# A second record of TensorE's activity, and zero matmuls by it, in a four-layer attention kernel

## The chip, the core and the metric

The kernel runs on one core of one Trainium2 chip, as one launch. A core has five engines that run at the same time, each through its own list of instructions: TensorE (PE in the profile; its weight loads are the row PEld), ScalarE (ACT), VectorE (DVE), GpSimd (POOL) and SyncE (SP, which here only issues DMAs). They wait for one another by semaphores. The metric is the device time of one execution in microseconds (us). TensorE's clock is not constant: the profile has a record of the share of the full clock that was granted, called the granted clock here.

## What is computed

Four layers act on x of 2048 tokens by 512 features (32 heads of 16 features), each adding to x. Layers 0 and 2 are kind A: causal softmax attention within segments of 512 tokens, plus a linear-attention memory of the earlier segments. Layers 1 and 3 are kind B: full softmax attention over all 2048 tokens.

```
x = x + A(layernorm(x)); x = x + B(layernorm(x))
x = x + A(layernorm(x)); x = x + B(layernorm(x))

B: q, k, v = split(x @ wqkv)
   p = softmax(q k^T * 0.25);  o = p v;  return o @ wo
A: per segment s of 512 tokens, with the running memory M, z:
   a_dot = softmax(q k^T * 0.25 + causal mask) v
   a_mem = (phi(q) M) / (phi(q) z + 1e-6)
   o = g * a_mem + (1 - g) * a_dot;  then M += phi(k)^T v, z += sum(phi(k))
   return o @ wo
```

Nearly all of the work is the exponentials: 32 heads by 2048 by 2048 scores in each B layer.

## The kernel before

Every instruction is recorded first, in Python, and only then written to the engines. The class `Sched` keeps for each engine a list of operations and a clock `t` of when the engine would be through by the kernel's own estimates (`estimate`, line 95). `add` (line 123) finds what an operation must wait for from the buffers and the PSUM banks it touches. `Builder.attention` (line 1759) decides the order by comparing these estimated clocks, so that whatever moves an estimated clock also moves the order of the rest. The constants of those decisions are replaced every 40 us or so of estimated time (`PIECES`, line 271).

The work is cut into groups (`Group`, line 227): one layer, one segment of 512 queries, one chunk of eight heads and one half of those heads. A group is a list of score blocks, each 128 keys by 512 queries of one head. The main loop runs in steps. Each step makes one unit (`unit`, line 1454):

- three score blocks on TensorE, each a matmul that uses 32 rows of the array (`ps<-qm,KA` or `ps<-qm,KB` in the profile), into three PSUM banks; two sets of three banks alternate,
- one or two ScalarE instructions that take the exponential of the banks into `pT` (line 1514),
- for kind A the causal mask on GpSimd (line 1529).

VectorE makes a part of the exponentials itself, in the tiles `dxw`, from score blocks that go to separate banks (lines 1121 and 1184). Two units later the value matmuls take `pT` and `dxw` into the accumulating bank `ACC` (`pv`, line 1556): in the last layers with 17 columns of the array and 512 streamed rows (`128*17`), else with the whole array and 34 or 51 rows. The list `pvq` holds what is still due, and `g.left` counts the value matmuls that a group still lacks. Projections, layer norms, the memory and the output projection are background tasks, run between units (`background`, `bg_one`) as far as the estimated clocks leave room. Q, K and V are held in SBUF; DMA transposes move `xn`, `ob`, `KA` and `amem` between their two layouts.

At the end of each step stands `keep_busy` (line 429). It adds matmuls whose weights are the all-zero tile `zero`, so that they add zero to the accumulating bank, or write to a free one when no group is accumulating. It does so while the recorded streaming time of TensorE in the last 3413 ns, kept in `streams`, is under the share `FILL`, and at most `FILLS` times a step. In `streams` a matmul on 32 rows counts 0.285 of its streaming time, one on 17 columns 0.38. These zeros go through `add` like any other matmul: they move TensorE's estimated clock and so what the builder does next. All matmuls are recorded in one helper, `mm`, at line 445. A zero matmul shows in the profile as `ps<-wB,zero`.

Of the kernel before, what the change touches and what calls it, by code (L numbers as in the profile page):

```python
# [22 lines left out]
UNIT, DXB, ACC = (0, 4), 3, 7  # L23
# [6 lines left out]
class Op:  # L30
    __slots__ = ("eng", "idx", "fn", "deps", "emit", "evno", "is_dma", "batch", "name", "end")

    def __init__(self, eng, idx, fn, name=""):
        self.eng = eng
        self.idx = idx
        self.fn = fn
        self.deps = []
        self.emit = False
        self.evno = None
        self.is_dma = False  # L40
        self.batch = None
        self.name = name
        self.end = 0.0
# [35 lines left out]
class Sched:  # L79


    def __init__(self):
        self.ops = {e: [] for e in ENGS}
        self.t = {e: 0.0 for e in ENGS}
        self.tiles = []

        self.streams = []

    def streamed(self, until, ns):

# [4 lines left out]
    def estimate(self, op, ns, gap, tile):  # L95
        e = op.eng
        ready = max([d.end + LAG[d.eng] if d.eng != e else d.end + 35 for d in op.deps], default=0.0)
        if tile is not None:
            rows, r0, cols, c0, n = tile
            st = max(ready, self.pe_issue())  # L100
            if cols < 128:
                st = max(st, self.pe_issue() + 30)
            for i, (a, ar, b, bc, m, at) in enumerate(self.tiles):
                if ar < r0 + rows and r0 < ar + a and bc < c0 + cols and c0 < bc + b:
                    after = 104 if (a, b) != (rows, cols) else 5 if cols == 128 else 4
                    if after == 5 and rows == 128 and 0 < i == len(self.tiles) - 1 and self.tiles[i - 1][0] == 32:
                        after += 13
                    st = max(st, at + m / 2.4 + after)
            self.tiles = self.tiles[-11:] + [(rows, r0, cols, c0, n, st)]
            self.t["pe"] = max(self.t["pe"], st + n / 2.4)  # L110
            self.streams.append((st, n / 2.4 * (0.285 if rows < 128 else 0.38 if cols < 128 else 1)))
            op.end = st + n / 2.4 + 170
        elif e == "sp":
            st = max(ready, self.t[e])
            self.t[e] = st + max(gap, 600)
            op.end = st + ns
        else:
            op.end = self.t[e] = max(self.t[e] + gap, ready + ns)
# [139 lines left out]
class Builder:  # L258
# [170 lines left out]
    def keep_busy(self):  # L429


        g, n = self.cur, 0
        own = g is not None and g.npv
        if not own and (self.bank_late() > 0 or any(t["next"][0][:1] == ["cont"] for t in self.tasks)):
            return
        bank, al = (self.banks[ACC], g.acc) if own else (self.banks[DXB], self.new_alloc())
        soon = [w.end + LAG[w.eng] for e in self.pvq[:9] if e[0] <= self.unit_no + 1 for w in (self.b_pT[e[4] * 3 + e[5]].last_write,)]
        at = max(self.sc.t["act"] - 1330, min(soon, default=0.0) - self.HOR)
        while n < self.FILLS and self.sc.streamed(max(self.sc.t["pe"], at), 3413) < self.FILL:
            self.mm(self.ps[:, bank.col0:bank.col0 + 512], self.zero[:, :], self.wB[:, 0, 0:512], not own, not own,  # L440
                    [self.b_zero, self.b_wB[0]], bank, al, "fill")
            n += 1

    def mm(self, out, lhsT, rhs, start, stop, reads, bank, alloc, name="", tile=(128, 0, 128, 0), n=512):
        self.sc.add("pe", lambda e: e.matmul(out, lhsT, rhs, start=start, stop=stop, skip_group_check=True),  # L445
                    reads=reads, banks=[(bank, "w", alloc)], name=name, tile=tile + (n,))
# [1312 lines left out]
    def attention(self):  # L1759
        self.flags = {("x", 0, s) for s in range(NSEG)} | {"amem"}  # L1760
        self.xT_free = [0, 1]
        self.dma_at, self.forcing = {}, False
        self.sel, self.pvq, self.deferred, self.qm_free = [], [], [], [0, 1, 2, 3]
        self.qm_late = []

        self.dx_use, self.dx_bufs = [0] * (self.NDX + self.NAREA), list(range(self.NDX))
        self.areas, self.dx_open = self.dx_areas(), set()
        self.dx_build, self.dx_pairs, self.dx_now, self.dxq, self.dx_own = [], [], [None] * self.CHAINS, [], []
        self.dx_seen, self.wide, self.dx_todo = set(), False, 0
        self.wt = set()  # L1770
        self.dx_shut, self.dx_gone = set(), set()
        self.dx_step = self.bank_step = -9
        self.bubble = True
        self.forced, self.low, self.cur, self.gap = 0, True, None, 1
        self.pend = None
        self.nfin, self.oT_owner = {}, {}
        self.cr_pe = self.cr_dve = 0
        self.running, self.filling = None, False
        self.step = self.bg_cols = 0
        self.misc_banks = [DXB]  # L1780
        self.unit_no = 0
        self.parts = {}
        self.pieces = list(self.PIECES)
        self.make_groups()
        self.make_tasks()
        n = 0
        while True:
            items = self.take_banks(2)
            if not items:
                if not self.seqA and not self.seqB and len(self.tasks) == self.CHAINS:  # L1790
                    self.last_out(n)
                    break

                if self.pvq or self.pend:
                    self.step += 1
                    self.pv_step(n + 9, True)
                    self.run_deferred(False)
                    continue
                self.misc_banks = [DXB, 0, 1, 2, 4, 5, 6]
                self.bubble = True  # L1800
                if not self.bg_one():
                    assert self.deferred, ("stuck", [t["next"] for t in self.tasks])
                    self.run_deferred(True)
                continue
            self.misc_banks = [DXB]
            if self.bubble:
                self.bubble, self.cr_pe, self.cr_dve = False, 0, 0
            self.step += 1
            while self.pieces and self.sc.t["act"] >= self.pieces[0][0] * 1000:
                self.__dict__.update(self.pieces.pop(0)[1])  # L1810
            self.near = self.ahead()
            self.dx_widen()
            self.low = self.near < self.LOW
            self.gap = self.GAP if self.near >= self.AHEAD else 1
            isA = items[0][0].kind == "A"
            split = not self.low and not isA
            self.unit_no = n
            self.units = n
            early = self.pend is not None or self.ends(0)
            first = self.pv_step(n) if early else 0  # L1820
            self.compose(n, items)
            self.credit(self.PE_LOW if self.low else self.PE_A if isA else self.PE_B, self.CR_LOW if self.low else self.CR_A if isA else self.CR_W * len(items) / 3 if self.wide else self.CR_B)
            if split and (not self.FIT or not self.wide or self.FIT & 2):
                self.background(True)
            self.cr_dve -= first if early else self.pv_step(n)
            self.run_deferred(False)
            self.background(False if split and not (self.FIT & 1 and self.wide) else None)
            if self.step == 2:
                self.gates()
            left = sum(len(g.banks) - g.pos for g in self.sel)  # L1830
            if not self.seqA and not self.seqB and left <= 3 and not self.parts and len(self.tasks) == self.CHAINS and self.met([("dma", ("oT", 3, 3, c)) for c in range(NCH - 1)]):
                self.last_part(1, self.banks[DXB])
            elif self.step > 10:
                self.keep_busy()
            self.bg_cols = 0
            n += 1

# [48 lines left out]
```

## Time and profile before

| | |
|---|---|
| median of 3 runs | 1772.71 us (1769.92 to 1774.93) |
| the profiled execution, its own time | 1774.13 us |
| its span, first to last instruction | 1772.3 us |
| mean granted TensorE clock | 0.994 |
| ScalarE busy | 1729.2 us, 98% |
| TensorE busy (matmul rows) | 1586.6 us, 90% |
| VectorE busy | 1521.1 us, 86% |
| GpSimd busy | 287.2 us, 16% |
| matmul rows in the profile / weight loads | 17251 / 17436 |
| zero matmuls, by their weight loads | 177 |

A row of the timeline gives start, length, engine, line, operation and tiles, and in brackets how long the engine stood idle before it. Neighbouring matmuls overlap in these rows, and a matmul's end is modelled, so starts are more to be trusted than lengths. A row of the windows gives a stretch of the span, its length, the busy time (with the number of instructions) of PE, PEld, DVE, ACT and POOL, and then the granted clock, the DMA share and GB/s. A row of the waits says which engine and line waited for which, with the total in us, how often, and the longest. Some matmul rows are missing (185 of 17436 here); the weight loads are complete.

### The profile page before, as it was taken

The numbers are of one execution on the slowest core, as the hardware profiler recorded it, in microseconds if no ns is written. First come the engines' busy times: TensorE is split into PE (matmuls) and PEld (weight loads), VectorE is DVE, ScalarE is ACT, GpSimd is POOL, SyncE is SP. The second block draws the span as 40 slices with busy tenths as digits, with TensorE's granted clock in tenths as the row PEclk, the third lists the DMA queues.
The fourth block names the chain that finished last, engine by engine and source line by source line (L and its number), as shares of the span: only waits on it lengthen the run. The fifth ranks groups of instructions, "written<-read, shape, count | busy, mean of one in ns | idle before, by whom it ended". The sixth has DMA issues, their size and how long they took to land.

```text
span 1772.3 us, 42500 instructions
## 1 busy us (share of the span) xinstructions
PE 1586.6 (90%) x17251; PEld 568.1 (32%) x17436; DVE 1521.1 (86%) x3001; ACT 1729.2 (98%) x1674; POOL 287.2 (16%) x656
## 2 busy tenths in 40 slices
PE   7889898889898989989989988988898898889988
PEld 4445454553224222233222332332222222222222
DVE  6677766589995999888999879768999999999997
ACT  7989998999999999999999999999999999999998
POOL 4622515110006000113000240141100000000000
PEclk9999998999999999999999999999999999999999
DMA  6021111000001000000000010110000000000000
GB/s 173 20 46 29 32 20 25 14 9 7 13 7 16 4 13 13 2 19 14 8 13 13 5 34 7 19 26 13 2 13 1 1 7 7 1 1 7 7 1 13
DMA packets 86180, 30.01 MB, mean 17 GB/s; under 512 B 78816, under 2 KB 85472, under 8 KB 85984
## 3 DMA queue, kind: packets, MB, share of 16 engines
q1 hardware_dynamic: 85984, 27.29, 7.6%
q8 instruction: 136, 2.23, 0.5%
q14 instruction: 60, 0.49, 0.1%
HBM read 6.30 MB, written 2.10 MB: 5 GB/s over the span
## 4 chain that ended last, share of the span: by engine, by line
ACT 52%; PE 22%; issue 17%; DVE 6%; POOL 2%; DMA 1%; SPq 0%; ACTq 0%; DVEq 0%; POOLq 0%
ACT pT L1514 51%; PE ps L445 22%; POOL pT L1529 2%; DVE QA L1121 1%; ACT amem L697 0%; DVE dxw L1184 0%; DVE dxw L1121 0%; DMA xT<-xn 0%; DVE rg L809 0%; DVE VB L1121 0%; DVE VB L480 0%; DVE KA L1646 0%; DVE VA L1184 0%; DVE ob L1628 0%; DVE phq L700 0%
## 5 line engine op out<-in xcount | busy, mean ns | idle before, releaser
L1514 ACT ACTIVATE pT<-ps 128x1024 bf16<-128x1024 f32 (+4 forms) x1623 | 1697.0, 1201 | 27.8 <-PE ps L445 21.0
L445 PE MATMUL ps<-qm,KB 32*128 32x512 bf16 x3584 | 517.8, 384 | 79.0 <-ACT pT L1514 67.3
L445 PE MATMUL ps<-pT,VB 128*17 128x512 bf16 x2221 | 377.7, 384 | 8.7 <-ACT pT L1514 3.7
L1529 POOL TENSOR_SCALAR_AFFINE_SELECT pT<-pT 128x256 bf16<-128x256 bf16 (+2 forms) x524 | 213.0, 418 | 548.4 <-ACT pT L1514 535.9
L445 PEld LDWEIGHTS ps<-qm,KB 32*128 32x128 bf16 x3584 | 131.6, 91 | 458.1 <-ACT pT L1514 355.1
L1424 POOL TENSOR_SCALAR qm<-QB,par 128x512 bf16<-128x512 bf16 x88 | 66.9, 763 | 848.7 <-PE ps L445 769.4
L445 PEld LDWEIGHTS ps<-pT,VB 128*17 128x17 bf16 x2221 | 88.1, 87 | 240.0 <-issue 202.5
L1121 DVE TENSOR_SCALAR dxw<-ps 128x512 uint16<-128x512 f32 (+1 forms) x212 | 145.4, 697 | 4.5 <-PE ps L445 3.6
L445 PE MATMUL ps<-qm,KA 32*128 32x384 bf16 (+3 forms) x1024 | 104.3, 307 | 26.0 <-ACT pT L1514 19.5
L1121 DVE TENSOR_SCALAR VA<-ps 128x512 uint16<-128x512 f32 (+1 forms) x172 | 121.4, 720 | 5.8 <-PE ps L445 4.7
L1184 DVE TENSOR_SCALAR dxw<-dxw 128x1024 uint16<-128x1024 uint16 (+1 forms) x302 | 121.0, 411 | 3.5 <-PE ps L445 1.7
L1121 DVE TENSOR_SCALAR QA<-ps 128x512 uint16<-128x512 f32 (+1 forms) x168 | 117.8, 716 | 4.9 <-PE ps L445 4.1
L445 PE MATMUL ps<-qm,QA 32*128 32x512 bf16 x512 | 103.6, 384 | 19.9 <-ACT pT L1514 18.6
L445 PE MATMUL ps<-VA,pT 128*128 128x51 bf16 (+1 forms) x2560 | 108.6, 188 | 14.1 <-POOL pT L1529 6.5
L445 PE MATMUL ps<-dxw,VW 128*17 128x512 bf16 x437 | 108.7, 381 | 0.2 <-DVE dxw L1184 0.2
L445 PEld LDWEIGHTS ps<-VA,pT 128*128 128x128 bf16 x2560 | 85.6, 97 | 63.8 <-POOL pT L1529 30.3
L1121 DVE TENSOR_SCALAR VB<-ps 128x512 uint16<-128x512 f32 (+1 forms) x117 | 92.1, 804 | 2.8 <-PE ps L445 2.1
L1121 DVE TENSOR_SCALAR KB<-ps 128x512 uint16<-128x512 f32 (+1 forms) x98 | 77.9, 808 | 2.5 <-PE ps L445 2.1
L445 PE MATMUL ps<-pT,VA 128*17 128x512 bf16 x386 | 76.7, 384 | 2.2 <-ACT pT L1514 1.8
L445 PE MATMUL ps<-dxw,VB 128*17 128x512 bf16 x256 | 74.1, 381 | 0.0
L445 PE MATMUL ps<-VB,pT 128*128 128x34 bf16 (+1 forms) x1788 | 69.4, 186 | 2.0 <-ACT pT L1514 1.1
L445 PE MATMUL ps<-xT,wB 128*128 128x512 bf16 x224 | 63.0, 393 | 5.8 <-issue 2.7
(292 smaller groups left out, 2408.1 us busy)
## 6 DMA issues: line engine op xcount, KB each, us to landing
out_dram<-x SPq DMA_DIRECT2D x8, 256.0 KB, 2.1
x<-in_A_x_dram SPq DMA_DIRECT2D x3, 512.0 KB, 5.1
wB<-in_B_wqkv_dram SPq DMA_DIRECT2D x1, 1536.0 KB, 11.7
xT<-xn SPq DMA_TRANSPOSE x60, 2.4
oT<-ob SPq DMA_TRANSPOSE x36, 2.4
x<-in_A_x_dram SPq DMA_DIRECT2D x4, 128.0 KB, 2.7
wA<-in_A_wq_dram SPq DMA_DIRECT2D x1, 512.0 KB, 5.1
wA<-in_A_wk_dram SPq DMA_DIRECT2D x1, 512.0 KB, 6.1
```

The source lines that it names most:

```text
L445: self.sc.add("pe", lambda e: e.matmul(out, lhsT, rhs, start=start, stop=stop, skip_group_check=True), reads=reads, banks=[(bank, "w", all ...
L1121: self.sc.add("dve", lambda e: e.tensor_scalar(d, o, SCALE * LOG2E * 128, W_C if dxs[0][:3] in self.wt else EXP_C, op0=ALU.mult, op1=ALU.add),
L1184: self.op("dve", lambda e: e.tensor_scalar(o, w, d, None, op0=ALU.add), reads=self.b_dxw[b0][:len(ents)], writes=wr, ns=(295, 425, 560, 69 ...
L1424: self.op(eng, (lambda m, q, col: lambda e: e.tensor_scalar(m, q, col, 0.0, op0=ALU.mult, op1=ALU.add))(m, q, col), reads=[bq, self.b_par] ...
L1514: self.sc.add("act", (lambda dst, src: lambda e: e.activation(dst, src, ACT.Exp, scale=SCALE))(dst, src), writes=self.b_pT[slot * 3 + i:sl ...
L1529: self.op("pool", (lambda blk, pat: lambda e: e.affine_select(blk, blk, pattern=pat, compare_op=ALU.is_ge, fill=0.0, base=0, channel_multi ...
```

## The change

`Sched` gets a second record, `rows`, beside `streams`, filled in `estimate`: for each matmul its start and a weight. A matmul on fewer than 128 rows counts 0.3 of its streaming time; those on fewer than 128 columns count 0.85 of the time in which at least one of them streams (`fm_end` holds how far that reaches); whole-array matmuls count in full, or 0.9 when they stream under 100 rows. A new method, `quiet`, runs at the end of each step after `keep_busy`. It sums `rows` over the 3413 ns ahead of the later of two estimated times, TensorE's clock and ScalarE's less 1330 ns. If the sum is under 0.57 of 3413 ns, and a group has begun to accumulate and is not finished, it records one zero matmul of 512 rows into `ACC`. It then puts back the estimated clocks, the list of recent tiles and `streams` to what they were, so no later decision sees this matmul; `rows` keeps it.

In the programs, 244 zero matmuls are added (421 in place of 177), at most one at the end of a step. All other instructions of the five engines stand in their old order.

```diff
-        self.streams = []
+        self.streams, self.rows, self.fm_end = [], [], 0.0
...
             self.streams.append((st, n / 2.4 * (0.285 if rows < 128 else 0.38 if cols < 128 else 1)))
+            if rows < 128:
+                w = 0.3 * n / 2.4
+            elif cols < 128:
+                w = 0.85 * max(0.0, st + n / 2.4 - max(st, self.fm_end))
+                self.fm_end = max(self.fm_end, st + n / 2.4)
+            else:
+                w = n / 2.4 * (0.9 if n < 100 else 1)
+            self.rows = [r for r in self.rows[-400:] if r[0] >= st - 7000] + [(st, w)]
...
+    QUIET = 0.57
+
+    def quiet(self):
+
+        sc, g = self.sc, self.cur
+        at = max(sc.t["pe"], sc.t["act"] - 1330)
+        if g is None or not g.npv or g.left == 0 or sum(w for t, w in sc.rows if t >= at - 3413) >= self.QUIET * 3413:
+            return
+        held = dict(sc.t), list(sc.tiles), list(sc.streams)
+        bank = self.banks[ACC]
+        self.mm(self.ps[:, bank.col0:bank.col0 + 512], self.zero[:, :], self.wB[:, 0, 0:512], False, False, [self.b_zero, self.b_wB[0]], bank, g.acc, "quiet")
+        sc.ops["pe"][-1].end = held[0]["pe"]
+        sc.t, sc.tiles, sc.streams = held
...
             elif self.step > 10:
                 self.keep_busy()
+                self.quiet()
```

## The prediction

> **What bounds the kernel now.** The page first, for the share of each engine, the chain that ended last and the costliest group.
>
> ```profile
> span 1772.3 us, 42500 instructions
> PE 1586.6 (90%) x17251; PEld 568.1 (32%) x17436; DVE 1521.1 (86%) x3001; ACT 1729.2 (98%) x1674; POOL 287.2 (16%) x656
> ...
> ACT 52%; PE 22%; issue 17%; DVE 6%; POOL 2%; DMA 1%; SPq 0%; ACTq 0%; DVEq 0%; POOLq 0%
> ...
> L1514 ACT ACTIVATE pT<-ps 128x1024 bf16<-128x1024 f32 (+4 forms) x1623 | 1697.0, 1201 | 27.8 <-PE ps L445 21.0
> ```
>
> ScalarE's exponentials (L1514) fill the span; TensorE can gain or lose time only where ScalarE waits for its scores. The span is not one regime, so the windows by stage came next, then the chain of the first stage and the waits of TensorE and of ScalarE in the last two.
>
> ```profile
> 0.00:360.00 360.00, 312.46 (x4653) 174.01 (x4712) 242.47 (x598) 332.53 (x331) 128.37 (x309) 0.97 0.21 44
> 360.00:1380.00 1020.00, 925.20 (x9365) 305.92 (x9480) 902.36 (x1813) 1011.64 (x991) 146.16 (x331) 1.00 0.06 12
> 1380.00:1772.30 392.30, 348.96 (x3238) 88.14 (x3244) 376.29 (x592) 385.00 (x354) 12.69 (x16) 1.00 0.02 5
> ```
>
> The columns are the stretch, then busy time of PE, PEld, DVE, ACT and POOL, then the granted clock. ScalarE stands idle 27.5 of the first 360 us, 8.4 of the next 1020, 7.3 of the rest (the drain at the end is in that). The first fence is the chain of 0 to 360 us, the others what the engines waited for in 360 to 1380 us and from 1380 us.
>
> ```profile
> by line: PE ps L445 33.4%; ACT pT L1514 31.3%; issue 13.3%; POOL pT L1529 4.7%; DMA xT<-xn 2.0%; ACT amem L697 1.2%; DVE dxw L1121 1.0%; DVE VB L480 1.0%; DMA x<-in_A_x_dram 0.9%; DVE dxw L1184 0.9%; DVE phq L700 0.7%; DVE x L911 0.6%; DVE
> ```
>
> ```profile
> PE ps L445 <- ACT pT L1514: 63.4, 191, 1.2
> ```
>
> ```profile
> PE ps L445 <- ACT pT L1514: 32.9, 98, 0.6
> ACT pT L1514 <- PE ps L445: 0.9, 4, 0.3
> ```
>
> So a third of the first stage's chain is TensorE's; after 360 us TensorE is the one that waits (63.4 and 32.9 us for ScalarE to free score banks), while from 1380 us on ScalarE waits for scores only 0.9 us.
>
> **What there is to win.** The mean granted clock is near one.
>
> ```profile
> core 0: 1772.3 us, clock 0.994
> ```
>
> The clock fell to half four times before the end. Windows of 3.4 us on the grid of those falls show each fall (0.50 in the clock column) and the window ahead of it; the rows of 81.50 and 300.00 us are windows of the same grid with little TensorE work and no fall behind them.
>
> ```profile
> 40.60:44.00 3.40, 1.43 (x26) 0.84 (x24) 2.22 (x5) 3.40 (x3) 1.06 (x3) 1.00 0.19 39
> 44.00:47.40 3.40, 3.18 (x23) 1.33 (x23) 0.69 (x1) 2.97 (x5) 1.70 (x4) 0.50 0.00 0
> 88.40:91.80 3.40, 2.02 (x37) 1.10 (x36) 3.33 (x10) 3.25 (x5) 2.71 (x7) 1.00 0.72 82
> 91.80:95.20 3.40, 2.74 (x14) 1.05 (x16) 1.62 (x6) 1.27 (x2) 1.06 (x4) 0.50 0.56 113
> 102.00:105.40 3.40, 1.70 (x14) 0.73 (x15) 2.44 (x6) 2.75 (x3) 2.28 (x5) 1.00 0.77 84
> 105.50:108.90 3.40, 3.23 (x29) 1.73 (x29) 1.70 (x5) 2.14 (x2) 0.00 (x0) 0.50 0.00 0
> 276.10:279.50 3.40, 2.33 (x49) 1.61 (x50) 3.23 (x8) 3.40 (x6) 2.85 (x6) 1.00 0.00 0
> 279.50:289.70 10.20, 9.78 (x97) 4.93 (x99) 4.87 (x14) 6.97 (x10) 5.31 (x15) 0.50 0.42 53
> ```
>
> ```profile
> 81.50:85.00 3.50, 2.38 (x50) 1.70 (x49) 2.76 (x9) 3.50 (x5) 2.34 (x7) 1.00 0.35 72
> 300.00:303.40 3.40, 2.25 (x29) 1.03 (x27) 2.72 (x6) 2.79 (x3) 1.98 (x5) 1.00 0.00 0
> ```
>
> In the half-clock rows ScalarE is idle 0.43, 2.13, 1.26 and 3.23 us, together 7.05 us: the most that an unbroken clock can return in this execution. The first stage loses 27.5/360 = 7.6% anyway, 1.6 of these 20.4 us, so some 5.5 us belong to the clock, 1.9 of them to the second fall and 2.4 to the fourth. No fall stands after 290 us.
>
> The Trainium skill (TensorE: Matmul & The Clock Gate, the section on HAM oscillation) puts the danger at TensorE gaps of more than about 3.4 us. This trace does not agree: TensorE worked 1.43 to 2.33 of the 3.40 us ahead of each fall. By that rule the zeros would be useless here, which is a rival below. In its Terms the Trainium skill, on the same page, prices throttled time at (1 - K/N) of it, an estimate of 10.2 us for these 20.4 us at half clock; the trace has 7.05 us of idle ScalarE at most and decides, and by the page's price in place of it, with the same share of it gained, the sum below would be 1.5 us lower.
>
> **The change part by part.** In program order the changed kernel has 244 zero matmuls more (421 against 177), every other instruction of all five engines in its old order, and no DMA moved. The bookkeeping costs nothing on the chip. Matched with the weight loads of this trace, 42 of the 244 fall before 360 us, 134 in 360 to 1380, 68 after; 132 have the narrow value matmuls (17 columns wide) as a neighbour, 65 of them in the second stage and 67 in the third. Most stand just ahead of a unit's score matmuls (`qm`).
>
> What one takes of TensorE is read off the zeros that are there already, in TensorE's timeline.
>
> ```profile
> 612.28 0.39 PE L445 MATMUL ps<-pT,VB 128*17 128x512 bf16 x2
> 612.60 0.39 PE L445 MATMUL ps<-wB,zero 128*128 128x512 bf16 x1
> 612.92 0.39 PE L445 MATMUL ps<-qm,KB 32*128 32x512 bf16 x3
> ```
>
> ```profile
> 1539.70 0.38 PE L445 MATMUL ps<-QA,VA 128*17 128x512 bf16 x1
> 1540.02 0.38 PE L445 MATMUL ps<-qm,KB 32*128 32x512 bf16 x1
> ```
>
> ```profile
> 308.58 0.26 PE L445 MATMUL ps<-VW,dxw 128*128 128x51 bf16 x4
> 308.81 0.60 PE L445 MATMUL ps<-qm,KB 32*128 32x512 bf16 x3
> ```
>
> ```profile
> 1044.45 0.38 PE L445 MATMUL ps<-VA,pT 128*128 128x51 bf16 x8
> 1044.66 0.38 PE L445 MATMUL ps<-wB,zero 128*128 128x512 bf16 x1
> 1044.97 0.39 PE L445 MATMUL ps<-qm,KB 32*128 32x512 bf16 x3
> ```
>
> Between narrow value matmuls and scores the step is 0.32 us without a zero and 0.64 with one: 0.32 us each. After full-width value matmuls, eight take 0.21 us to the zero and 0.31 more to the scores, 0.52; four take 0.23 without a zero, so eight some 0.33: about 0.2 us each. On TensorE that is 132 x 0.32 + 112 x 0.2 = 65 us: 42 x 0.2 = 8.4 in the first stage, 65 x 0.32 + 69 x 0.2 = 34.6 in the second, 67 x 0.32 + 0.2 = 21.6 in the third. It is queued ahead of the scores, and ScalarE waits for those; VectorE's share of the exponentials waits for them too. All of it on the path would be +65 us; but in the last two stages TensorE waited 63.4 and 32.9 us for ScalarE, more than the zeros take. The cover fails where a zero stands at a start that was not waiting. Rows of 40 us show what ScalarE has lost to zeros so far; the second fence is the zeros alone, whose PEld count says how many there are.
>
> ```profile
> 540.00:580.00 40.00, 31.33 (x483) 15.86 (x490) 24.02 (x59) 39.09 (x42) 22.99 (x57) 1.00 0.12 18
> 620.00:660.00 40.00, 36.25 (x323) 10.03 (x324) 38.46 (x82) 40.00 (x40) 1.57 (x3) 1.00 0.07 15
> 940.00:980.00 40.00, 38.19 (x319) 11.09 (x323) 38.04 (x77) 39.84 (x41) 0.00 (x0) 1.00 0.10 15
> ```
>
> ```profile
> 540.00:580.00 40.00, 6.42 (x20) 1.86 (x27) 0.00 (x0) 1.00 0.12 18
> 620.00:660.00 40.00, 0.39 (x1) 0.29 (x3) 0.00 (x0) 1.00 0.07 15
> 940.00:980.00 40.00, 0.00 (x0) 0.00 (x0) 0.00 (x0) 1.00 0.10 15
> ```
>
> Twenty-seven zeros stand where ScalarE lost 0.91 us; 940 to 980, with none, lost 0.16; so at most 0.75/27 = 0.028 us each. 620 to 660, with three, lost nothing. The new ones stand at about five per 40 us, nearer the second row, so I take 0.01 us, with 0 and 0.028 as ends: 202 x 0.01 = 2.0 us after 360 us (0 to 5.7). In the first stage I take the chain's share of TensorE, 0.334 x 8.4 = 2.8 us (0 to 8.4).
>
> The gain: matched with the trace, one new zero stands in the window ahead of the second fall and one ahead of the fourth, none ahead of the first and third. One adds some 0.2 us: 2.33 becomes about 2.54, above the 2.25 and 2.38 that did not fall, so I count the fourth as gone (2.4); 2.02 becomes 2.23, on the line, so half of the second (0.9). Together -3.3 us, ends 0 and -7.05.
>
> Sum: 2.8 + 2.0 - 3.3 = +1.5 us on the profiled execution's 1774.13, which is 1.4 us over the median of the runs, 1772.71. On the median that is 1774.2 us.
>
> **The rivals.**
> - Slower: the third stage has no slack. VectorE is busy 376.29 of its 392.30 us and ScalarE 385.00, and the zeros' 21.6 us need two thirds of TensorE's 32.9 us of waiting. If half of them stand where TensorE was not waiting, 10.8 us go to scores that are late; ScalarE waited only 0.9 us there, so little absorbs it. 1774.2 + 10.8 less what I already count there (0.7) is 1784. Against it: the waits are many and short (98), so most delays meet one soon. It decides from about 4 us of new ScalarE idle in that stage (1778.0 less 1774.2).
> - Faster: all four falls go and the zeros are covered throughout: 1772.7 - 7.05 = 1765.7, and 1767 with a microsecond of zeros on the path. For it: TensorE's waiting is larger than the zeros. Against it: two falls have no new zero ahead of them.
> - The change doesn't do what it says: falls come as before, since a window is lifted by only one zero. 1774.2 + 3.3 = 1777.5, still within 0.3%; with the first stage's whole 8.4 paid it is 1783. For it: two falls have no new zero ahead of them and a third only reaches the line. Against it: all four falls followed low windows. The Trainium skill's rule on gaps (TensorE: Matmul & The Clock Gate, the section on HAM oscillation) would have it so; the windows ahead of the falls speak against the rule.
>
> **How the numbers follow.** About 0.3% (5.3 us) is what a measurement of this kernel can tell from no change: its three runs spread from 1769.92 to 1774.93. My forecast, gain and cost near each other, has 0.36, and the change without effect on the clock 0.12; of that, 0.04 lies above 1778.0, where the first stage pays in full. So same has 0.44. The late third stage has 0.32: slower 0.36. Faster has 0.20. The ends of the terms give 1774.13 - 7.05 - 1.42 = 1765.7 and 1774.13 + 8.4 + 5.7 - 1.42 = 1786.8; leaving out 2 in 10 the range is 1766 to 1785. The forecast's own range is 1770 to 1778.
>
> **What would show it.** `wB,zero` weight loads 421; the granted clock above 0.994, with no stretch at 0.50 near 280 us; ScalarE's idle time of 0 to 360 us below 27.5; TensorE's wait for ScalarE after 360 us lower by most of the zeros' 56 us. Wrong would be: ScalarE waiting several microseconds for scores after 1380 us (the slower rival), or the clock at 1.00 throughout and ScalarE's time unchanged (the faster one).

## The result and the profile after

The changed kernel takes 1787.19 us, the median of 5 runs (1786.37 to 1787.75), against 1772.71 us: ratio 1.0083, interval 1.0068 to 1.0098. It is 14.5 us slower; forecast was 1.5 us slower with a range that ended at 1785. The profiled execution took 1787.01 us, its span is 13.0 us longer than before.

The page of the changed kernel, with the rows that answer to those shown of before (its line numbers are 22 higher from `mm` on):

```profile
span 1785.3 us, 42931 instructions
...
PE 1620.9 (91%) x17438; PEld 580.9 (33%) x17680; DVE 1524.6 (85%) x3001; ACT 1734.0 (97%) x1674; POOL 285.9 (16%) x656
...
ACT 49%; PE 27%; issue 16%; DVE 6%; POOL 1%; DMA 1%; ACTq 0%; DVEq 0%; POOLq 0%; SPq 0%
...
L1536 ACT ACTIVATE pT<-ps 128x1024 bf16<-128x1024 f32 (+4 forms) x1623 | 1701.4, 1178 | 36.1 <-PE ps L467 25.7
```

TensorE's share of the chain went from 22% to 27%. ScalarE's 1623 exponentials take 1701.4 us of the span where they took 1697.0, although one lasts 1178 ns in the mean where it lasted 1201: 1623 x 1201 less 1697 was 252 us of overlap between one record and the next, now it is 211 us. Most of these 41 us, 1623 x 23 ns or 37 us, is only that each record is shorter; the other 4.4 us are more busy time. So a late unit costs ScalarE in two ways: its idle time before these instructions grew by 8.3 us (27.8 to 36.1), and its busy time by 4.4, which a row of busy time doesn't show as idle.

All engines but TensorE run the same instructions in the same order, so ScalarE's 1674 instructions of the two profiles can be matched one to one. By their ends the changed kernel was 3.9 us ahead where the kernel before stood at 360 us, 10.2 behind at 1380, and 13.0 behind at the end. The windows of the changed kernel that hold the same work as the three stages of before:

```profile
0.00:356.10 356.10, 314.04 (x4687) 173.30 (x4754) 243.64 (x598) 332.58 (x331) 127.60 (x309) 1.00 0.20 45
356.10:1390.20 1034.10, 950.46 (x9476) 314.11 (x9609) 903.70 (x1813) 1015.14 (x991) 145.59 (x331) 1.00 0.06 12
1390.20:1785.30 395.10, 356.43 (x3279) 93.54 (x3317) 377.27 (x592) 386.25 (x354) 12.68 (x16) 1.00 0.02 5
```

The second stage grew from 1020.0 to 1034.1 us; ScalarE's idle time in it from 8.4 to 19.0. The waits of that stage, TensorE's for ScalarE and ScalarE's for TensorE, first before, then after:

```profile
PE ps L445 <- ACT pT L1514: 63.4, 191, 1.2
```

```profile
ACT pT L1514 <- PE ps L445: 6.2, 16, 1.0
```

```profile
PE ps L467 <- ACT pT L1536: 48.2, 153, 0.9
```

```profile
ACT pT L1536 <- PE ps L467: 13.7, 37, 1.2
```

TensorE took 34.6 us of zeros more in this stage by the prediction's count, but its waiting for ScalarE fell only by 15.2 us. The stage is 14.1 us longer, so a large part of the rest pushed its other work back, and 37 exponentials waited for scores where 16 had.

One such place, in TensorE's and ScalarE's timelines. Before:

```profile
782.12 0.39 PE L445 MATMUL ps<-pT,VB 128*17 128x512 bf16 x2
782.66 0.38 PE L445 MATMUL ps<-wB,zero 128*128 128x512 bf16 x1 [0.16 <-issue]
782.97 0.39 PE L445 MATMUL ps<-qm,KB 32*128 32x512 bf16 x3
```

```profile
780.61 6.15 ACT L1514 ACTIVATE pT<-ps 128x1024 bf16<-128x1024 f32 x6
```

And after:

```profile
782.97 0.39 PE L467 MATMUL ps<-pT,VB 128*17 128x512 bf16 x2
783.29 0.82 PE L467 MATMUL ps<-wB,zero 128*128 128x512 bf16 x3
784.05 0.39 PE L467 MATMUL ps<-qm,KB 32*128 32x512 bf16 x3
```

```profile
781.20 2.98 ACT L1536 ACTIVATE pT<-ps 128x1024 bf16<-128x1024 f32 x3
784.54 3.28 ACT L1536 ACTIVATE pT<-ps 128x1024 bf16<-128x1024 f32 x3 [0.36 <-PE ps L467]
```

From the value matmuls to the scores it was 0.85 us, with two old zeros, which the builder had entered in its estimated clocks (one is missing from the rows); with the added one it is 1.08 us. ScalarE, which ran without a break there, now waits 0.36 us.

The granted clock rose as was forecast, from 0.994 to 0.998 in the profiles. Its falls before the end stand at 102.0 and at 1184.0 us in the changed kernel, each 3.4 us long, and the one near 280 us is gone from this profile:

```profile
102.00:105.40 3.40, 3.04 (x24) 1.37 (x23) 1.40 (x4) 1.46 (x2) 0.00 (x0) 0.50 0.01 1
...
278.00:288.50 10.50, 9.37 (x149) 5.15 (x147) 7.45 (x17) 9.94 (x14) 6.95 (x19) 1.00 0.33 63
...
1184.00:1187.40 3.40, 3.18 (x29) 1.50 (x26) 1.87 (x4) 2.12 (x3) 2.35 (x4) 0.50 0.18 37
```

### The profile page after: what moved, and what is told of

It is laid out like the page before. It is cut to its first block, busy times and chain, and to the rows that moved or that the text cites. A ratio compares the mean times of both kernels' runs of the same rounds, so it can differ in the third digit from the quotient of the medians.

```text
span 1785.3 us, 42931 instructions
## 1 busy us (share of the span) xinstructions
PE 1620.9 (91%) x17438; PEld 580.9 (33%) x17680; DVE 1524.6 (85%) x3001; ACT 1734.0 (97%) x1674; POOL 285.9 (16%) x656
## 4 chain that ended last, share of the span: by engine, by line
ACT 49%; PE 27%; issue 16%; DVE 6%; POOL 1%; DMA 1%; ACTq 0%; DVEq 0%; POOLq 0%; SPq 0%
ACT pT L1536 48%; PE ps L467 27%; POOL pT L1551 1%; DVE VB L1143 1%; DMA phq<-amem 0%; DVE dxw L1143 0%; DMA xT<-xn 0%; DVE dxw L1206 0%; DVE ob L1650 0%; ACT amem L719 0%; DVE QA L1143 0%; DVE VB L502 0%; DVE KA L1668 0%; DVE VA L502 0%; DVE amem L844 0%
## 5 line engine op out<-in xcount | busy, mean ns | idle before, releaser
L1536 ACT ACTIVATE pT<-ps 128x1024 bf16<-128x1024 f32 (+4 forms) x1623 | 1701.4, 1178 | 36.1 <-PE ps L467 25.7
L467 PE MATMUL ps<-qm,QA 32*128 32x512 bf16 x512 | 102.1, 386 | 17.3 <-ACT pT L1536 14.3
L467 PE MATMUL ps<-wB,zero 128*128 128x512 bf16 x297 | 100.7, 385 | 3.2 <-issue 2.0
```

What stands on the lines that cost most here:

```text
L1536: self.sc.add("act", (lambda dst, src: lambda e: e.activation(dst, src, ACT.Exp, scale=SCALE))(dst, src), writes=self.b_pT[slot * 3 + i:sl ...
```

## The experiments

**Two measures.** Falls of the clock lie in other places in each profile, and the time goes with the mean clock: the runs of the kernel before beside these experiments go from 1768.0 us at a mean clock of 0.998 to 1776.9 at 0.990. So beside the ratio stands the time at equal clock. It is a fit of straight lines in the mean granted clock, one slope for all kernels and a height for each, through the spans and clocks of all runs; the kernel without its own zeros and the reckoned one, the last below, are left out. The slope is 1.04 us for each 0.001 of mean clock (give or take 0.04), and the fit leaves some 0.85 us of scatter. The second measure comes from the profiles: how much longer ScalarE took from the end of one matched instruction to the end of the next, summed over a stage without the falls of either kernel (each with 3 us behind it). Over stretches without an added or a missing zero it comes out between -0.9 and 0.7 us, so about 1 us is what it can tell from nothing. By it the changed kernel loses 15.3 us after 360 us and 1.0 before, outside falls; in falls it gains 4.9 us before 360 us and loses 1.6 after.

**The theory** after the result: a zero costs what it takes of TensorE, less what TensorE would have waited there, less the lead by which that unit's scores were ready before ScalarE needed them. **The rivals**: every zero after 360 us costs alike; the price is one per instruction, not one of streaming; the price comes from leaving the zeros out of the reckoning.

In the first four kernels `quiet` decides as before and enters each zero in `rows`, but issues only those of a set, so that the places of the others don't move.

```diff
-        self.mm(..., "quiet")
-        sc.ops["pe"][-1].end = held[0]["pe"]
+        self.nquiet += 1
+        if self.kept(self.nquiet - 1):
+            self.mm(..., "quiet")
+            sc.ops["pe"][-1].end = held[0]["pe"]
+        else:
+            sc.estimate(Op("pe", 0, None), 300, 215, (128, 0, 128, 0, 512))
```

**Only the early 42** (`kept`: `i < 42`).

> Only the first 42 of the 244 added zeros, those before 360 us; the other 202 are reckoned in the second record but not issued. Theory (late scores): the early zeros cost ScalarE nothing and take away falls of the clock, so the whole gain of 3.9 us that the changed kernel had over the one before at 360 us stays: 1772.7 - 3.9, about 1769, with fewer than four falls of the clock. Rival (the early gain is only where the falls happened to lie in those two executions): 1772 to 1773, the falls as often as before.

1775.13 us, ratio 1.0008, interval 0.9994 to 1.0023. No gain: at equal clock they cost 3.3 us (give or take 0.6), and the mean clock, 0.9948 where the runs of before beside them had 0.9931, gives back 1.8. In the profile they cost 0.9 us before 360 us outside falls, so the two measures differ here. The 3.9 us that the changed kernel was ahead at 360 us was in good part chance: the profile of before with its four falls is one of the slower ones, and the profiles of the next six kernels below, none of which has the early 42, are 1.6 to 7.1 us ahead of it there. The rival came nearer. A fall came at 275.4 us, close to where the fourth stood before, with more busy TensorE ahead of it:

```profile
272.00:275.40 3.40, 2.42 (x48) 1.39 (x47) 2.94 (x7) 3.40 (x5) 2.10 (x5) 1.00 0.00 0
275.40:278.80 3.40, 3.18 (x37) 2.04 (x38) 1.94 (x4) 2.10 (x5) 1.62 (x4) 0.50 0.04 10
```

**Only the thin 39**, those after 360 us where the scores of the unit behind the zero had been ready under 0.3 us ahead (`i >= 42 and i in THIN`), and **only the other 163** (`i >= 42 and i not in THIN`).

> Only 39 of the 202 zeros after 360 us: those ahead of a unit whose scores, in the trace of the kernel before, were ready less than 0.3 us before ScalarE finished the unit ahead of it. Theory (late scores): these carry most of the loss; their own units lost 8.7 us between the two traces, and with a share of the units behind them 9 to 11: 1782 to 1784. Rival (every late zero costs alike, 17 us over 202): 39 x 0.084 = 3.3 us, 1776.

> The other 163 zeros after 360 us, ahead of units whose scores were ready 0.3 us or more early. Theory (late scores): 3 to 6 us, 1776 to 1779, though they are four times as many as in the run of 39. Rival (every late zero costs alike): 163 x 0.084 = 13.7 us, 1786.

39 zeros: 1780.93 us, ratio 1.0042 (1.0026 to 1.0058), 8.5 us at equal clock, 8.6 outside falls by the profile, a little under the 9 to 11 expected: 0.22 us each, about what a zero takes of TensorE (0.2 to 0.32 us). 163 zeros: 1778.02 us, 1.0033 (1.0021 to 1.0044), 6.9 and 6.4 us, a little over the 3 to 6 expected: 0.04 us each. The uniform price (3.3 and 13.7) falls; the lead tells the two apart by five to one. It isn't that the 39 stand among the narrow matmuls, where a zero takes more: 18 of the 39 have one just ahead, and 129 of the 163.

**All 202 late ones** (`i >= 42`).

> All 202 zeros after 360 us and none of the early 42. Both theories: 1772.7 + 17 = 1790, with the early falls of the clock back. If it comes out at 1787 instead, the early zeros bring nothing; if the sum of the runs of 39 and of 163 is far from it, their delays are not independent.

1780.74 us, ratio 1.0050 (1.0032 to 1.0068), 9 us under what was expected. The clock explains 4 us of that: these runs had 0.9969 in the mean against 0.9931 of before beside them. Some 3.6 us more is the price: at equal clock the 202 zeros cost 13.4 us, outside falls 13.7 by the profile, where 17 had been taken, with one fall of the changed kernel in it. The rest is within the spread of these seven runs (1778.75 to 1787.50). The two parts come to 15.0 by the profile (8.6 + 6.4), near the whole; and at equal clock the late ones' 13.4 and the early ones' 3.3 come to 16.7 of the changed kernel's 18.2. Why the clock of these runs was higher isn't shown: the profile of before has no fall between 360 us and the end that a late zero could take away.

ScalarE's waits for scores after 360 us in these profiles (the first row is the kernel before, then the 163, the 39 and the 202):

```profile
ACT pT L1514 <- PE ps L445: 7.1, 20, 1.0
```

```profile
ACT pT L1544 <- PE ps L475: 8.6, 24, 1.0
```

```profile
ACT pT L1544 <- PE ps L475: 12.8, 33, 1.2
```

```profile
ACT pT L1544 <- PE ps L475: 15.0, 41, 1.2
```

The next two put the zeros in by a list of places in TensorE's order, into the kernel before, after everything is recorded.

```diff
+            if k in at:
+                ops.append(Op("pe", 0, lambda e: e.matmul(bank, self.zero[:, :], self.wB[:, 0, 0:512],
+                                                          start=False, stop=False, skip_group_check=True), "added"))
             ops.append(op)
```

**119 zeros where TensorE had waited**, and **119 where it had not**.

> The kernel before with 119 zeros of 512 rows put in after 360 us, by a list of places and not by a record: each ahead of scores for which TensorE had stood idle 0.24 us or more in the trace of before. Theory (a zero costs what it takes of TensorE less what TensorE would have waited there and less ScalarE's lead): 0 to 2 us at equal clock, so 1772 to 1774 with perhaps a fall of the clock less. Rival (every late zero costs alike, 13.4 us over 202 at equal clock): 119 x 0.066 = 7.9 us, 1779 to 1781.

> The kernel before with as many zeros, 119 after 360 us, each between narrow value matmuls and scores at a place where TensorE had stood idle less than 0.02 us. Theory: each delays its scores by 0.32 us; ScalarE's lead there (a quarter of the places under 0.29 us, the median 0.44) hides most of some and none of others: 7 to 12 us at equal clock, 1779 to 1784, several times the run at idle places. Rival (every late zero costs alike): the same as the run at idle places.

At waits: 1773.53 us, ratio 1.0005 (0.9994 to 1.0016); 1.8 us at equal clock, 1.2 outside falls, near what the measures can tell from nothing: 0.01 us each. Elsewhere: 1788.60 us, 1.0090 (1.0069 to 1.0111); 17.5 and 17.3 us: 0.15 us each, above the range I gave. The same number of the same instruction costs ten to fourteen times as much, by its place alone. The neighbours are nearly alike (108 of the 119 places at waits are behind narrow value matmuls, all 119 of the others). The places lie otherwise over the stages, 63 and 56 in the second and third at waits, 90 and 29 elsewhere, but each stage by itself shows the contrast: 1.2 us against 14.7 in the second, nothing against 2.6 in the third, outside falls. ScalarE's waits for scores after 360 us, at waits and elsewhere:

```profile
ACT pT L1526 <- PE ps L457: 7.4, 21, 1.0
```

```profile
ACT pT L1526 <- PE ps L457: 16.6, 51, 1.0
```

7.4 us is close to the 7.1 that the kernel before had; 16.6 is more than twice that. The 9.5 us between is only part of the 17 us; the rest doesn't show as a wait.

**Without 102 of the old zeros.** Of the zeros of `keep_busy` after 360 us into the accumulating bank, those that no other instruction waits for are entered in the builder's clocks as before and then taken out of TensorE's list, so that the order stays.

```diff
+        fills = lambda o: o.name == "fill" and o.own and not o.emit and o.at > 360000
+        self.sc.ops["pe"] = [o for o in self.sc.ops["pe"] if not fills(o)]
         self.sc.finalize()
```

> The kernel before without 102 of its own reckoned zeros after 360 us, everything else in its order. If a reckoned zero cost what the prediction read from the rows (at most 0.028 us), this gains at most 2.9 us at equal clock and loses some of it to more falls of the clock: 1772 to 1776. If it cost what the unreckoned ones cost after 360 us (0.066 us), it gains 6.7 us at equal clock, 1767 to 1770.

1782.31 us, ratio 1.0064 (1.0047 to 1.0081): slower, outside both expectations. The clock fell for 82 us after 360 us, and the mean was 0.975. Three of these falls, the first with the window ahead of it:

```profile
537.80:541.20 3.40, 1.60 (x31) 0.89 (x29) 1.78 (x4) 3.40 (x5) 2.17 (x6) 0.99 0.19 39
541.20:548.00 6.80, 6.80 (x77) 3.99 (x78) 2.32 (x6) 6.19 (x7) 4.43 (x11) 0.50 0.01 2
558.20:575.30 17.10, 15.56 (x151) 5.89 (x147) 10.79 (x21) 14.63 (x15) 7.17 (x18) 0.50 0.08 16
1039.50:1060.00 20.50, 19.75 (x165) 6.46 (x163) 16.62 (x31) 17.33 (x17) 6.37 (x13) 0.50 0.19 27
```

In the falls the kernel lost 14.4 us; outside them, after 360 us, 0.3 us (about half a us either way, by where a fall's end is put): taking zeros out gained nothing. Of the 102, 76 stood outside falls; at the new zeros' 0.066 us they would have given back 5 us. So the old zeros were free, as far as this shows, and worth about 14 us by the clock they hold. The price of 0 to 0.028 us that the prediction read from the rows was right for them.

**Short zeros**, 64 streamed rows in place of 512 in all 244 places.

```diff
-        self.mm(self.ps[:, bank.col0:bank.col0 + 512], self.zero[:, :], self.wB[:, 0, 0:512], ...
+        self.mm(self.ps[:, bank.col0:bank.col0 + 64], self.zero[:, :], self.wB[:, 0, 0:64], ...
```

> The changed kernel with its 244 added zeros streaming 64 rows instead of 512, in the same places. Theory (the price is TensorE's time): a zero takes some 0.03 us between full-width matmuls instead of 0.2, and 0.13 between narrow ones and scores instead of 0.32, about a third of the 65 us: 5 to 7 us at equal clock instead of 18, 1777 to 1781 with falls of the clock as before. Rival (a price per instruction, by its weight load or its place in the queue): 18 us at equal clock, 1787 and more.

1773.44 us, ratio 1.0010 (0.9999 to 1.0022): 4.4 us at equal clock and 4.1 after 360 us outside falls, a quarter of the whole zeros' 18.2 and 15.3, and less than the 5 to 7 expected. So some three quarters of the price or more is TensorE's streaming time, and not one per instruction. The time came out under the expected 1777, with a better clock in the runs (0.9966) than was allowed for.

**Zeros at waits, the early stage too**: 91 places, 80 before 360 us, several at one place where the wait holds them.

> The kernel before with 91 zeros at places chosen from its trace: 80 before 360 us (as many at a place as TensorE's wait there holds, and six ahead of units whose scores were ready early), 11 at waits of TensorE around 550, 830, 1045 and 1170 us. No other change of order. Theory: they cost 0 to 2 us at equal clock and lift the windows of little activity; of the 6 to 7 us that the falls of the clock cost the kernel before (1.03 us for each 0.001 of mean clock), a third to a half comes back: 1769 to 1771, ratio 0.998 to 0.999. Rival (zeros before 360 us cost as the 42 did, 0.08 us each, wherever they stand): 91 x 0.08 = 7 us less 3 of clock, 1776 to 1777.

1771.19 us, ratio 0.9997 (0.9988 to 1.0006): no difference, between the two expectations. The clock is held, 0.9985 in the mean and nearly the same in each run (1769.85 to 1772.51); after 360 us the zeros cost 1.1 us outside falls. But before 360 us they cost 2.8 us there, and all of them 3.7 us at equal clock, against the 0 to 2 expected, and that takes up most of what the clock gave. Why zeros at TensorE's waits cost something in this stage, and next to nothing after it, was not tried further. I have no version that beats the kernel before.

**Reckoned**: the three lines that keep and put back the estimates are left out.

```diff
-        held = dict(sc.t), list(sc.tiles), list(sc.streams)
...
-        sc.ops["pe"][-1].end = held[0]["pe"]
-        sc.t, sc.tiles, sc.streams = held
```

> The changed kernel without the lines that put the estimated clocks back, so the builder sees its added zeros as it sees the old ones; the order of the rest moves, and 356 zeros are added instead of 244. Theory A (the price comes from their being left out of the reckoning: the builder goes on placing background work as if TensorE were free): cost per added zero well under the 0.074 us of the changed kernel, 356 x 0.02 = 7 us or less, 1772 to 1780. Theory B (the second record asks for zeros where TensorE is not waiting, and counting them does not help): 356 x 0.074 = 26 us at equal clock, 1793 or more.

1854.20 us, ratio 1.0464 (1.0449 to 1.0480), far over both theories. ScalarE's waits for scores over the whole span:

```profile
ACT pT L1533 <- PE ps L464: 71.0, 127, 3.5
```

The builder then makes another order (1683 ScalarE instructions in place of 1674, 356 zeros added), so the 82 us are not the zeros' price alone. It can't tell whether leaving the zeros out of the reckoning is what makes the change slow; it says only that counting them in, under constants set for another order, is worse. The two runs of 119 zeros speak against that rival: none of theirs was in the reckoning, and by their place they cost 1.2 or 17.3 us.

## Why the prediction was wrong

- **The price of a zero after 360 us** is the step that failed: 0.01 us taken, with 0 and 0.028 as ends, 2.0 us for 202. Measured: 13.4 us at equal clock, 13.7 in the profile outside falls, 0.066 us each. The rows it was read from (27 old zeros in 540 to 580 us) were read rightly: taking such zeros out changed next to nothing. They were no rows for the new ones, whose price goes by their places. In the trace of before, TensorE was idle for less than 0.05 us just ahead of the matmul behind the zero at 143 of the 244 places, 114 of them after 360 us; the prediction matched the places with the trace to count them by stage and did not look at the waits there. The second record's rule can pick such places: its sum counts score matmuls at 0.3, so that it is low while TensorE has no pause. Why the old zeros were free stays open. They are entered in the builder's clocks, and the rest is ordered after them; but their sum counts scores at 0.285 in the same way, and in the run without the 102, TensorE was idle for less than 0.05 us at 42 of the 76 different places where they had stood (several at some), so pauses there aren't the whole of it.
- **The cover in the last two stages** (63.4 and 32.9 us of waiting against 34.6 and 21.6 us of zeros) was a sum over stages. At the places themselves it was often not there: 39 of the 202 cost as much as the other 163 and more. Of the 56 us of waiting that the zeros were to take up, they took 21.3 (15.2 in the second stage, 6.1 in the third).
- **What a zero takes of TensorE** (0.2 and 0.32 us, 65 us in all) agrees with the runs, which don't measure it by itself: the dearest places cost 0.22 us each, and zeros an eighth as long a quarter as much.
- **The first stage** was put at 2.8 us: 3.3 at equal clock, but only about 1 in the profiles outside falls (1.0 in the changed kernel, 0.9 with the early 42 alone).
- **The clock** was put at -3.3 us, and the size came out: by the fit the changed kernel's runs have 0.997 against 0.9938, worth 3.3 us. That it came by the forecast's way isn't shown, and the match is in part luck. The early 42, to which the whole gain was put down, raised the clock by 0.0017 in their own runs (1.8 us); the 202 late ones, to which none was, had 0.0038 (4.0 us) in theirs. The reading of the windows was weak as well: it took 2.25 and 2.38 us of busy TensorE as safe, while a fall had followed 2.33, and with the early 42 one followed 2.42.
- **The slower rival** had the mechanism, late scores, and nearly the size (1784), but the wrong stage: it looked for the loss after 1380 us, where ScalarE and VectorE are fullest. That stage lost 2.8 us, the one ahead of it 14.1. **That the zeros leave the clock alone** fits badly with the clocks: 0.997 in the changed kernel against 0.9938, 0.9985 with 91 zeros at waits against 0.9943 beside it, and 0.975 without the 102 old ones. **The faster rival** is refuted by the result.

## What to carry to other kernels

Filler work is priced by its places, not by its number: before adding some, look in the trace, place by place, at how long the engine waited there and how early its result was ready for the bound engine. The price of filler that is already there says little of new filler that another rule places: here 102 old zeros cost nothing that could be measured, and 202 new ones 13.4 us. And where an execution's clock falls at changing times, compare kernels at equal clock, over many runs; two profiles alone showed a gain of 3.9 us at 360 us that the runs of the early zeros didn't.

## What the runs showed of the hardware

A microsecond at half clock costs far less than half a microsecond here: 0.001 of the mean clock is 3.5 us at half clock in a span of 1771, and cost 1.04 us, 0.3 for each; in the kernel without its old zeros it was 14.4 us for 82, 0.18 for each. That fits with ScalarE being busy for 98% of the span, but was not tried by itself. The Trainium skill (TensorE: Matmul & The Clock Gate, Terms) puts the penalty at (1 - K/N) of the throttled time, 0.5 for each at half clock, which is more than either; here the measurements decide.

Ahead of the falls shown here TensorE was not idle for a whole window: it was busy for 1.43 to 2.33 of 3.40 us ahead of the four in the prediction's rows, and for 1.60 in the row of 537.80 us above; in the row of 541.20 us it is busy for 6.80 of 6.80 at half clock, and the clock stays down for both windows. What of TensorE's work holds the clock is not told apart by these runs. With zeros of 64 rows the one profile had seven windows of fall after 360 us where the changed kernel's had one, but the mean clock over the runs is nearly the same, 0.9966 (10 runs) and 0.997 (5 runs).
